# Weight chunks made straight from the raw weights, and one index search for both halves of a head

## The chip, the cores and the metric

The kernel runs on one core of a Trainium2 chip. The metric is device time in microseconds from one launch to its end. Five engines work side by side, each through its own list of instructions in a fixed order: TensorE (PE, whose weight loads are listed as PEld), VectorE (DVE), ScalarE (ACT), GpSimd (POOL) and SyncE (SP, which issues most DMAs).

## The reference

A layer sums an attention part and a part with 4096 small experts, over 2048 tokens of width 512.

```python
xn = _layernorm(x)
out = x + _A_ref(xn, wq, wk, wv, wo) + _B_ref(xn, w_q, k1, k2, u, v)

# A: 32 heads of 16 for the queries, one shared head for keys and values
scores = einsum("bhqd,bkd->bhqk", q, k) * Dh ** -0.5
o = einsum("bhqk,bkd->bhqd", softmax(scores), v)      # then @ wo

# B: for each token and each of 32 heads, with dk = 128 and E = 64
s1 = einsum("nhd,ed->nhe", q1, k1)                     # 64 scores, first half
s2 = einsum("nhd,ed->nhe", q2, k2)                     # 64 scores, second half
i1, i2 = the two best of each;  t1, t2 their scores
cand = t1 + t2 (four sums);  the best two of these name two experts i1 * 64 + i2
g = softmax(of the two sums)
act = gelu(xn . u[expert])
out += g * act * v[expert]
```

## The kernel before

**Two streams.** The attention is a loop of 256 steps, each with eight `sc` products (L450), four exponentials (L457) and the `pv` products (L467). Its units set the pace. A second stream, the score thread, is dealt in between the steps: a fixed amount of its estimated cost (`yield` values, in us) for each step, so that it ends with the attention. All lists of instructions are written out ahead by this program; nothing is reordered at run time.

**The score thread** works on items. An item is one tile of 128 tokens times one chunk of four expert heads: twelve `psc` products (L701) give 128 x 512 scores in PSUM, eight groups of 64 (four heads, two halves). VectorE finds the eight largest of each group (L714, MAX8) and their places (L716, which the chip runs as a load of the eight values and a find). Four items make a `batch`: VectorE adds up the pair sums, POOL turns the places (`fi`, L760) into expert numbers, ACT takes an exponential and VectorE forms the gates. There are 128 items and 32 batches.

**The weight chunks.** The scores need w_q and the keys multiplied together, 512 x 512 for each of eight chunks. `wp_make` (L630 to 670) does this: for each of four heads two products `pw` (L646) with the keys `kTs` as the stationary side, a copy to SBUF by ACT (`wt`, L647), then for each quarter of the depth four transposes `pwt` (L659), from which ACT (L661) and VectorE (L662) form a high and a low f16 half. Chunks 0 and 1 are made at the start, 2 to 7 among the items of the first token group. The raw weights come by `wp_load` (L607) into `wqt` tiles; `wp_square` (L617) and `wp_factors` (L624) give a scale for each chunk from their squares.

**Experts.** For half of the tokens (the first two groups) each chosen expert is one slot of 128 tokens: an indirect DMA on POOL gathers 128 rows of u and v (L1181), VectorE multiplies u with the tokens (a dot, L1193), four slots share a short chain (`gq`, `gy`, `ga`, L1202 to 1204, a tanh on ACT and `w`, L1216), and VectorE adds v times the weight to the sum (an add, L1228). There are 512 slots; line 1591 sets how many a step gets. For the other two groups all 4096 experts are computed: one-hot products first, then a dense stage of `pact` (L917) and `pout` (L1059) products with splits on ACT and VectorE.

So the run has a start, then making chunks beside items and slots (A), items and slots (B), the first one-hot part and dense stage, items and slots again (C1, C2), the second one-hot part and the last dense stage. The guard at L383 reads a flag on every engine and branches past a fallback.

Of the kernel before, what the change touches and what calls it, by code (L numbers as in the profile page):

```python
# [60 lines left out]
def tile_kernel(ctx, tc, x, wq, wkv, wo, wqT, kT, uv, ub, vb, out):  # L61
# [570 lines left out]
    def wp_make(c):  # L632

        wt = [big.tile([P, 2, 512], F32, name="wt", tag="da", bufs=2) for _ in range(2)]
        for h in range(4):
            for n in range(4 * c + h + 1, min(4 * c + h + 5, 4 * NC) if late[0] else 4):
                if ("raw", n // 4, n % 4) not in WC:
                    wp_load(n // 4, n % 4)
            if c == 2 and h > 1:
                wp_square()  # L640
            if c > 2 and h == 1:
                wp_factors()
            w = WC.pop(("raw", c, h))
            p = xtile("pw")
            for s in range(2):
                nc.tensor.matmul(p[s * E:(s + 1) * E, :], kTs[:, s, :], w[:, s, :], start=True, stop=True)  # L646
            nc.scalar.copy(wt[h // 2][:, h % 2, :], p)  # L647
            yield 0.9
        WC[c] = []
        if c == 2:  # L650
            yield 0.05
            wp_factors()
            yield 0.05
        for k in range(KC):
            for _ in range((0, 2, 1, 1)[k] if 1 < c < NC - 1 else 0):
                wp_square()
            p = xtile("pwt")
            for h in range(4):
                nc.tensor.transpose(p[:, h * P:(h + 1) * P], wt[h // 2][:, h % 2, k * P:(k + 1) * P], ident)  # L659
            wk = wk_tile()  # L660
            nc.scalar.activation(wk[:, 0, :], p, AF.Copy, scale=col(S_W + c))  # L661
            low = lambda p=p, wk=wk: nc.vector.scalar_tensor_tensor(wk[:, 1, :], p, col(S_W + c), wk[:, 0, :],  # L662
                                                                    op0=OP.mult, op1=OP.subtract)
            if c == 1 and late[0] is None:
                AFTER.append(low)
            else:
                low()
            WC[c].append(wk)
            (store if c > 1 else BULK.append)(lambda k=k, wk=wk: nc.sync.dma_start(d_w[c][:, k], raw(wk[:])))
            yield 0.45  # L670

# [9 lines left out]
    BT = 4  # L681

    def item(n_, ti, make=()):
# [5 lines left out]
        if jb == 0:  # L689
            m8 = small.tile([P, BT, 8, 8], F32, name="m8", bufs=1)  # L690
            i8 = small.tile([P, BT, 8, 8], U32, name="i8", bufs=1)
            M8[ph, c, b], I8[ph, c, b] = m8, i8
# [20 lines left out]
        for s in range(8):  # L713
            nc.vector.max(m8[:, jb, s, :], p[:, s * E:(s + 1) * E])  # L714
        for s in range(8):
            nc.vector.max_index(i8[:, jb, s, :], m8[:, jb, s, :], p[:, s * E:(s + 1) * E])  # L716
# [16 lines left out]
    def batch(ph, c, b):  # L733
# [3 lines left out]
        mv = m8.rearrange("p t (h s) k -> p t h s k", s=2)  # L737
        a1, a2, b1, b2 = mv[:, :, :, 0, 0], mv[:, :, :, 0, 1], mv[:, :, :, 1, 0], mv[:, :, :, 1, 1]
# [19 lines left out]
        fi = T("fi", F32, [P, BT, 8, 2])  # L758
        G_ = V if ph >= NSP and c == NC - 1 else nc.gpsimd
        G_.tensor_copy(fi, i8[:, :, :, 0:2])  # L760
        fv = fi.rearrange("p t (h s) k -> p t h s k", s=2)
# [4 lines left out]
        if ph < NSP:  # L766
# [12 lines left out]
            def gates():  # L779
                V.tensor_scalar(den, ex, 2.0 * XUP, 2.0 * XUP, op0=OP.mult, op1=OP.add)  # L780
# [29 lines left out]
        def gates():  # L810
            V.tensor_scalar(den, ex, 2.0, 2.0, op0=OP.mult, op1=OP.add)
# [764 lines left out]
    with tc.manual_schedule(engines=ENGINES):  # L1576
# [6 lines left out]
        for d in range(half + 24):  # L1583
# [71 lines left out]
            att_steps(d, mid, fill)  # L1655
        flush()
# [12 lines left out]
def build(nc, tc, args):  # L1669
    tile_kernel(tc, *args)  # L1670
# [33 lines left out]
```

## Time and profile before

| | |
|---|---|
| three timed runs | median 1787.16 us (1787.01 to 1787.59) |
| the profiled execution | 1783.53 us, span 1781.7 us |
| PE busy | 1690.9 us, 95% |
| VectorE busy | 1592.7 us, 89% |
| ScalarE busy | 1329.0 us, 75% |
| GpSimd busy | 680.8 us, 38% |
| mean granted TensorE clock | 0.994 |

Busy time on PE includes the tail of each product, so back-to-back products overlap in it: a `psc` product lasts 381 ns on the mean, while fifteen in a row take about 3.34 us. Read shares by stretch, not over the whole span. A row of instructions gives line, engine, operation, output and inputs with their shape, count, then busy time and mean ns, then idle time ahead of it and what ended it. A row of the time order gives start and length in us; where the start of the next row comes before the end of the last one, the two overlap in the pipeline.

### The profile page before, as it was taken

The numbers are of one execution on the slowest core, as the hardware profiler recorded it, in microseconds if no ns is written. First come the engines' busy times: TensorE is split into PE (matmuls) and PEld (weight loads), VectorE is DVE, ScalarE is ACT, GpSimd is POOL, SyncE is SP. The second block draws the span as 40 slices with busy tenths as digits, with TensorE's granted clock in tenths as the row PEclk, the third lists the DMA queues.
The fourth block names the chain that finished last, engine by engine and source line by source line (L and its number), as shares of the span: only waits on it lengthen the run. The fifth ranks groups of instructions, "written<-read, shape, count | busy, mean of one in ns | idle before, by whom it ended". The sixth has DMA issues, their size and how long they took to land.

```text
span 1781.7 us, 35035 instructions
## 1 busy us (share of the span) xinstructions
PE 1690.9 (95%) x11070; PEld 598.6 (34%) x11070; DVE 1592.7 (89%) x6367; ACT 1329.0 (75%) x1793; POOL 680.8 (38%) x893
## 2 busy tenths in 40 slices
PE   7989998999998889999999999999988899999998
PEld 3433333333333333333333333333333333333332
DVE  7748889999999977999998999999999779999995
ACT  6468787877776987888887666666669887777774
POOL 1024444445542002344343554545530124555450
PEclk9999999999999999999999999999999999999999
DMA  7378788999773469999999987767544679999993
GB/s 261 126 235 313 267 280 298 298 331 330 258 264 105 155 214 281 318 318 344 331 334 347 344 278 250 238 223 238 162 140 135 228 229 332 329 322 342 321 309 142
DMA packets 257272, 470.97 MB, mean 264 GB/s; under 512 B 107316, under 2 KB 118596, under 8 KB 257084
## 3 DMA queue, kind: packets, MB, share of 16 engines
q0 software_dynamic: 73728, 268.47, 43.7%
q1 hardware_dynamic: 182940, 199.59, 35.0%
q8 instruction: 87, 1.43, 0.3%
q14 instruction: 101, 0.83, 0.1%
q10 hardware_dynamic: 416, 0.66, 0.1%
HBM read 407.36 MB, written 56.39 MB: 260 GB/s over the span
## 4 chain that ended last, share of the span: by engine, by line
PE 47%; DVE 31%; ACT 8%; issue 4%; DMA 3%; SPq 1%; POOL 0%; ACTq 0%; DVEq 0%; POOLq 0%
PE pv L467 14%; PE sc L450 8%; PE pout L1059 8%; DVE i L716 7%; PE pact L917 7%; PE psc L701 5%; ACT pt L457 5%; DVE m L714 5%; DVE xa L1228 5%; DVE g L1193 4%; DVE oh L975 3%; PE pwo L567 2%; PE pw L646 1%; DVE obs L977 1%; DVE obs L978 1%
## 5 line engine op out<-in xcount | busy, mean ns | idle before, releaser
L457 ACT ACTIVATE pt<-sc 128x1024 f32<-128x1024 f32 x1024 | 990.2, 1026 | 327.6 <-PE sc L450 276.8
L1181 POOL DMA_INDIRECT g<-in_uv_dram,idx x512 | 550.3, 1075 | 867.2 <-DVE xa L1228 398.0
L467 PE MATMUL pv<-pt,vaug 128*32 128x512 f32 x4096 | 496.2, 602 | 0.0
L1228 DVE SCALAR_TENSOR_TENSOR xa<-g,w,xa 128x512 f32<-128x512 f32 x512 | 374.2, 747 | 0.1
L701 PE MATMUL psc<-wk,xt 128*128 128x512 f16 x1536 | 358.0, 381 | 7.8 <-DVE wk L662 4.7
L450 PE MATMUL sc<-qa,kaug 64*128 64x512 f16 x2048 | 323.1, 382 | 39.1 <-ACT pt L457 34.4
L1193 DVE CUSTOM_DVE_ANT_0 g<-g,xa 128x512 f32<-128x512 f32 x512 | 335.1, 684 | 12.6 <-DMA g<-in_uv_dram,idx 12.3
L701 PEld LDWEIGHTS <-xt 128*128 128x128 f16 x1536 | 141.2, 98 | 205.5 <-issue 57.2
L450 PEld LDWEIGHTS <-kaug 64*128 64x128 f16 x2048 | 82.9, 94 | 377.5 <-issue 373.5
L716 DVE FIND_INDEX8 i<-m,psc 128x8 uint32<-128x64 f32 x1024 | 206.9, 226 | 0.0
L467 PEld LDWEIGHTS pv<-pt,vaug 128*32 128x32 f32 x4096 | 107.3, 109 | 253.4 <-issue 253.4
L917 PE MATMUL pact<-xt,wk 128*128 128x512 f16 x768 | 181.9, 382 | 0.0
L1059 PE MATMUL pout<-wk,wd 128*128 128x512 f16 x768 | 175.8, 379 | 0.0
L714 DVE MAX8 m<-psc 128x8 f32<-128x64 f32 x1024 | 146.3, 217 | 6.5 <-PE psc L701 6.2
L1059 PEld LDWEIGHTS <-wd 128*128 128x128 f16 x768 | 73.1, 98 | 92.5 <-issue 8.1
L917 PEld LDWEIGHTS <-wk 128*128 128x128 f16 x768 | 69.1, 98 | 99.5 <-issue 27.1
L975 DVE TENSOR_TENSOR oh<-io,tr 128x2048 f16<-128x2048 f16 x64 | 78.0, 1218 | 4.9 <-PE pg L1013 4.8
L716 DVE MATCH_VALUE_LOAD i<-m,psc 128x8 f32 x1024 | 76.7, 75 | 0.0
L760 POOL CAST fi<-i 128x64 f32<-128x64 uint32 x30 | 8.2, 272 | 147.2 <-DVE i L716 143.7
L1062 DVE SCALAR_TENSOR_TENSOR da<-pout,cols,da 128x512 f32<-128x512 f32 x72 | 53.1, 745 | 6.3 <-PE pout L1059 4.9
L1132 DVE SCALAR_TENSOR_TENSOR gy<-gy,pact 128x512 f32<-128x512 f32 x60 | 40.9, 681 | 17.4 <-ACT gy L1131 17.4
L1131 ACT ACTIVATE gy<-pact,cols 128x512 f32<-128x512 f32 x60 | 41.7, 696 | 15.3 <-PE pact L917 14.4
(227 smaller groups left out, 1458.7 us busy)
## 6 DMA issues: line engine op xcount, KB each, us to landing
wk<-dw SPq DMA_DIRECT2D x96, 256.0 KB
wqt<-in_wqT_dram SPq DMA_DIRECT2D x32, 512.0 KB
un<-in_uv_dram SPq DMA_DIRECT2D x16, 1024.0 KB
ds<-wk SPq DMA_DIRECT2D x64, 256.0 KB
gates<-dg SPq DMA_DIRECT2D x64, 256.0 KB
wk<-ds SPq DMA_DIRECT2D x64, 256.0 KB
dg<-gst SPq DMA_DIRECT2D x14, 928.0 KB
dw<-wk SPq DMA_DIRECT2D x32, 256.0 KB
```

The source lines that it names most:

```text
L450: nc.tensor.matmul(p[:, b, :], kaug[o:o + 64, kc * P:(kc + 1) * P], QA[u][o:o + 64, i, :], start=True, stop=True)
L457: nc.scalar.activation(PT[u, kc, i], p, AF.Exp, scale=SCALE)
L467: nc.tensor.matmul(PV[u][32 * j:32 * j + 32, :], vaug[:, kc, :], pt[:, b, :], start=kc == 0, stop=kc == 15)
L701: nc.tensor.matmul(p, XT[kk][:, a, j * P:(j + 1) * P], WC[n_][kk][:, bb, :], start=n == 0, stop=n == 11)
L714: nc.vector.max(m8[:, jb, s, :], p[:, s * E:(s + 1) * E])
L716: nc.vector.max_index(i8[:, jb, s, :], m8[:, jb, s, :], p[:, s * E:(s + 1) * E])
L917: nc.tensor.matmul(p, us[:, a, k * P:(k + 1) * P], XT[k][:, c, :], start=n == 0, stop=n == 11)
L975: nc.vector.tensor_tensor(out=oa, in0=num(P), in1=bc(0, tb, P), op=OP.is_equal)
L1059: nc.tensor.matmul(p, wd[0][:, a, j * P:(j + 1) * P], vs[:, c, :], start=n == 0, stop=n == last)
L1181: nc.gpsimd.indirect_dma_start(out=gt, out_offset=None, in_=uv, in_offset=bass.IndirectOffsetOnAxis(ap=IDX[ph, c, ti][:, s:s + 1], axis=0))
L1193: nc.vector.tensor_tensor_reduce(u, u, XN[TPH * ph + ti], scale=1.0, scalar=0.0, op0=OP.mult, op1=OP.add, accum_out=a[:, i:i + 1])
L1228: nc.vector.scalar_tensor_tensor(acc, v, w[:, i:i + 1], acc, op0=OP.mult, op1=OP.add)
```

## The change

**Weights.** Chunks 2 to 7 are made by `wp_direct`. The raw weights are the stationary side and the keys the moving one, so that each of 32 products (four quarters of the depth, four heads, two halves) gives its 128 x 64 part of `pwt` in the place where it is wanted. The products `pw`, their copies and the transposes are gone for these chunks. A chunk's four raw tiles are kept until its last quarter; `wp_load` has eight buffers for them in place of five. The squares and loads are dealt out in other places.

**Search.** The eight values of a head's second half are written from slot 6 of sixteen, over the last two of the first half, and one `max_index` for the head looks for eight values (six and two) in 128 scores. Places of the second half then count from 64; `over` takes 64 off. Where a value of the second half is also in the first, the place comes out below 64: `most` keeps a mark of it, `met_flag` turns it into a flag, and at the end `build` reads the flag on every engine and, if it is set, runs the whole program again with the old search.

**Rates.** Line 1669 deals slots to steps at 2.7, 2.5 and 2.1 in place of 2.5, 2.3 and 1.75.

```diff
     def wp_load(c, h):
         n = 4 * c + h
-        if n < 2 or n > 7 and (n - 8) % 5 < 2:
+        if n < 2 or n > 7 and (n - 8) % 8 < 2:
             w = big.tile([P, 2, D], F32, name="wqt", tag="wqt", bufs=2)
...
+        elif (n - 8) % 8 < 5:
+            w = late[0].tile([P, 2, D], F32, name="wqt", tag="gy", bufs=3)
         else:
-            w = late[0].tile([P, 2, D], F32, name="wqt", tag="gy", bufs=3)
+            w = big.tile([P, 2, D], F32, name="wqt", tag="oh", bufs=3)
...
+    def wp_direct(c):
+        ahead = [(c + 1, h) for h in range(4)] if c < NC - 1 else []
+        WC[c] = []
+
+        def make(k):
+            p = xtile("pwt")
+            for h in range(4):
+                w = WC["raw", c, h]
+                for s in range(2):
+                    nc.tensor.matmul(p[:, h * P + s * E:h * P + (s + 1) * E], w[:, s, k * P:(k + 1) * P], kTs[:, s, :],
+                                     start=True, stop=True)
+            wp_halves(c, k, p)
...
+        make(0)
+        load(2)
+        yield 1.3
+        load(3)
...
+        make(1)
+        square()
+        yield 1.3
...
+    SECOND = 8 if exact else 6
+    most = const.tile([P, BT, 4, 2], F32, name="most")
...
         for s in range(8):
-            nc.vector.max(m8[:, jb, s, :], p[:, s * E:(s + 1) * E])
-        for s in range(8):
-            nc.vector.max_index(i8[:, jb, s, :], m8[:, jb, s, :], p[:, s * E:(s + 1) * E])
+            nc.vector.max(m8[:, jb, s // 2, SECOND * (s % 2):][:, :8], p[:, s * E:(s + 1) * E])
+        if exact:
...
+        else:
+            for h in range(4):
+                nc.vector.max_index(i8[:, jb, h, :8], m8[:, jb, h, :8], p[:, h * P:(h + 1) * P])
...
+        for s in range(2):
+            G_.tensor_copy(fv[:, :, :, s, :], i8[:, :, :, SECOND * s:SECOND * s + 2])
+        if not exact:
+            over = T("over", F32, [P, BT, 4, 2])
+            G_.tensor_scalar(over, fv[:, :, :, 1, :], float(E), -float(E), op0=OP.is_ge, op1=OP.mult)
+            G_.tensor_add(fv[:, :, :, 1, :], fv[:, :, :, 1, :], over)
+
+        def meet():
+            if not exact:
+                V.tensor_max(most, most, over)
...
-            make = wp_make(n + 1) if 0 < n < NC - 1 else iter(())
+            make = wp_direct(n + 1) if 0 < n < NC - 1 else iter(())
...
-                pos += (2.5 if len(IDX) < NC * TPH else 2.3 if 0 <= d - since < 20 else 1.75, 0, 0.25, 1.5, 0.5)[dense_on[0]]
+                pos += (2.7 if len(IDX) < NC * TPH else 2.5 if 0 <= d - since < 20 else 2.1, 0, 0.25, 1.5, 0.5)[dense_on[0]]
...
+            if d == half - 8 and not exact:
+                met_flag()
...
+    with tc.tile_pool(name="met", bufs=1) as met:
+        flag = met.tile([1, 1], I32, name="met")
+        tile_kernel(tc, False, flag, *args)
+        again = nc.values_load(flag[0:1, 0:1], min_val=0, max_val=1)
+        with tc.If(again != 0):
+            tile_kernel(tc, True, None, *args)
```

VectorE's list at an item of B before: eight MAX that wait only for PE, eight searches, then a dot (`ISA g,act`, with the read of its sum). In brackets stand the semaphores that an instruction waits for; DVE is the engine's own.

```order
L714 MAX m_5951<-psc 128x8 [waits PE_49]
L714 MAX m_5951<-psc 128x8 x7
L716 MAX_INDEX i_5952<-m_5951,psc 128x8 [waits DVE_49] x8
L1193 ISA g,act<-g,xa 128x512 [waits DMASW0_49]
L1193 ISA act 128x1
```

The end of the same item now:

```order
L777 MAX m_5879<-psc 128x8
L777 MAX m_5879<-psc 128x8 [waits DVE_49]
L777 MAX m_5879<-psc 128x8
L777 MAX m_5879<-psc 128x8 [waits DVE_49]
L784 MAX_INDEX i_5880<-m_5879,psc 128x8 x3
L784 MAX_INDEX i_5880<-m_5879,psc 128x8 [waits DVE_49]
L1271 ISA g,act<-g,xa 128x512 [waits DMASW3_49]
L1271 ISA act 128x1
```

Four searches are gone, and of each pair of MAX the second waits for the first; the value waited for is the one that the MAX just ahead sets. Before, the value that a search waited for was set by the MAX eight places ahead.

VectorE's list between two items of B before (`gq`, `gy` and `ga` are the chain of four slots):

```order
L1193 ISA g,act<-g,xa 128x512 [waits DMASW2_49]
L1193 ISA act 128x1
L1193 ISA g,act<-g,xa 128x512 [waits DMASW3_49]
L1193 ISA act 128x1
L1228 SCALAR_TENSOR_TENSOR xa<-g,w,xa 128x512
L1202 SCALAR_TENSOR_TENSOR gq<-act 128x4 [waits DVE_49]
L1203 SCALAR_TENSOR_TENSOR gy<-gq,act 128x4 [waits DVE_49]
L1204 TENSOR_TENSOR ga<-act,gg 128x4
```

And after, at the same place:

```order
L1271 ISA g,act<-g,xa 128x512 [waits DMASW5_49]
L1271 ISA act 128x1
L1271 ISA g,act<-g,xa 128x512 [waits DMASW6_49]
L1271 ISA act 128x1
L1294 SCALAR_TENSOR_TENSOR w<-gth,ga 128x4 [waits Activation_49]
L1271 ISA g,act<-g,xa 128x512 [waits DMASW7_49]
L1271 ISA act 128x1
L1306 SCALAR_TENSOR_TENSOR xa<-g,w,xa 128x512 [waits DVE_49]
L1280 SCALAR_TENSOR_TENSOR gq<-act 128x4 [waits DVE_49]
L1306 SCALAR_TENSOR_TENSOR xa<-g,w,xa 128x512
L1281 SCALAR_TENSOR_TENSOR gy<-gq,act 128x4 [waits DVE_49]
L1306 SCALAR_TENSOR_TENSOR xa<-g,w,xa 128x512
```

Three dots and three adds stand where two dots and one add stood.

PE's list in A before, one quarter's transposes among the `psc` products:

```order
L701 MATMUL psc<-wk,xt 128x512
L701 LDWEIGHTS xt
L701 MATMUL psc<-wk,xt 128x512
L659 MATMUL pwt<-ident,wt 128x128 [waits DVE_49]
L659 MATMUL pwt<-ident,wt 128x128 x3
L701 LDWEIGHTS xt
```

And after, a quarter's eight products, ahead of the attention's next `sc`:

```order
L764 LDWEIGHTS xt
L764 MATMUL psc<-wk,xt 128x512
L674 MATMUL pwt<-kTs,wqt 128x64 [waits DVE_49]
L674 MATMUL pwt<-kTs,wqt 128x64 x7
L451 LDWEIGHTS kaug [waits DMAHW6_49,DMAHW5_49,DMAHW4_49]
L451 MATMUL sc<-qa_203,kaug 128x512 [waits Activation_49]
```

The weight load of an f32 product is not a row of its own in the list.

More of the change, by code (lines that the diff above doesn't have):

```diff
@@ L60, in tile_kernel @@
 @with_exitstack
-def tile_kernel(ctx, tc, x, wq, wkv, wo, wqT, kT, uv, ub, vb, out):
+def tile_kernel(ctx, tc, exact, flag, x, wq, wkv, wo, wqT, kT, uv, ub, vb, out):
     nc = tc.nc
@@ new lines, in wp_direct, with load @@
+    def wp_direct(c):
[8 more added lines that the diff above has]
+                                     start=True, stop=True)
+            wp_halves(c, k, p)
+            if k == KC - 1:
+                for h in range(4):
+                    WC.pop(("raw", c, h))
+        def load(h, c=c):
+            if c + 1 < NC and ("raw", c + 1, h) not in WC:
+                wp_load(c + 1, h)
+        square = wp_square if ahead else lambda: None
+        if c == 2:
+            load(1)
+            wp_square()
+            yield 0.05
+            load(2)
+            wp_square()
+            yield 0.05
+            load(3)
+            wp_factors()
+            yield 0.05
+            yield 0.05
+        make(0)
+        load(2)
+        yield 1.3
+        load(3)
+        if c == 2:
+            square()
+        yield 0.05
+        make(1)
+        square()
+        yield 1.3
+        square()
+        yield 0.05
+        make(2)
+        square()
+        yield 1.3
+        if c > 2:
+            square()
+        yield 0.05
+        if ahead:
+            wp_factors()
+        make(3)
+        yield 1.3
+        load(0, c + 1)
+        load(1, c + 1)
+        yield 0.05
@@ L681, in tile_kernel, with met_flag @@
     BT = 4
+    SECOND = 8 if exact else 6
+    most = const.tile([P, BT, 4, 2], F32, name="most")
+    nc.vector.memset(most, -float(E))
+    def met_flag():
+        m = small.tile([P, 1], F32, name="mm", bufs=1)
+        nc.vector.reduce_max(m, most.rearrange("p t h k -> p (t h k)"), axis=AX.X)
+        p = xtile("pm")
+        nc.tensor.transpose(p[:1, :P], m, ident)
+        r = small.tile([1, 1], F32, name="prd", bufs=1)
+        nc.vector.reduce_max(r, p[:1, :P], axis=AX.X)
+        nc.vector.tensor_scalar(flag, r, 0.0, None, op0=OP.is_ge)
     def item(n_, ti, make=()):
@@ L779, in gates @@
             def gates():
+                meet()
                 V.tensor_scalar(den, ex, 2.0 * XUP, 2.0 * XUP, op0=OP.mult, op1=OP.add)
@@ L810, in gates @@
         def gates():
+            meet()
             V.tensor_scalar(den, ex, 2.0, 2.0, op0=OP.mult, op1=OP.add)
```

52 lines of the change are left out of this document (20 added, 32 removed).

## The prediction

> **What bounds the kernel now.** I read the engine totals first, then the span in seven stretches cut where the work changes, then single instructions in order of time, and the waits last.
>
> ```profile
> span 1781.7 us, 35035 instructions
> PE 1690.9 (95%) x11070; PEld 598.6 (34%) x11070; DVE 1592.7 (89%) x6367; ACT 1329.0 (75%) x1793; POOL 680.8 (38%) x893
> ```
>
> PE looks like the bound, but VectorE is close behind, and a mean over the span hides who waits where. The stretches say more (columns: window, its length, then busy time of PE, PEld, DVE, ACT and POOL):
>
> ```profile
> 123.00:350.00 227.00, 213.64 (x1324) 75.02 (x1324) 201.56 (x1032) 181.61 (x264) 103.37 (x133) 0.98 0.85 288
> 350.00:558.00 208.00, 204.46 (x1264) 69.33 (x1263) 204.99 (x1336) 155.38 (x210) 102.58 (x190) 1.00 0.83 281
> 558.00:1018.00 460.00, 429.50 (x3057) 150.65 (x3056) 412.58 (x948) 382.52 (x511) 146.74 (x134) 0.99 0.86 286
> 1018.00:1174.00 156.00, 156.00 (x931) 52.71 (x929) 151.29 (x893) 97.17 (x119) 78.51 (x108) 1.00 0.77 264
> 1174.00:1326.00 152.00, 150.98 (x941) 51.02 (x937) 149.17 (x985) 97.83 (x119) 75.11 (x144) 1.00 0.58 188
> 1326.00:1420.00 94.00, 78.95 (x975) 33.42 (x979) 85.13 (x154) 82.84 (x101) 11.65 (x8) 1.00 0.51 166
> 1420.00:1750.00 330.00, 328.27 (x1993) 110.65 (x1989) 298.52 (x743) 254.00 (x340) 148.48 (x136) 1.00 0.95 310
> ```
>
> The rows are, in order: A, where the weight chunks are still made (attention steps 1 to 32); B, items and expert slots without making (33 to 64); the first dense stage; C1 and C2, items and slots again (137 to 160, 161 to 184); the second one-hot part; the last dense stage. In A every engine has room. In B and C2 PE and DVE are both full: DVE idles 208.00 - 204.99 = 3.0 us in B and 2.8 us in C2, so work added to DVE there lengthens the stretch almost in full, and work taken from it alone gains nothing, since PE has only 3.5 and 1.0 us of room. In the last dense stage PE is full and DVE has 31 us to spare.
>
> PE hardly waits for DVE so far; this is the row that will grow if DVE becomes the longer engine (waits of PE in 350 to 558):
>
> ```profile
> PE psc L701 <- DVE i L716: 2.2, 2, 1.1
> ```
>
> **The change, the search.** One item searches eight groups of 64. Before, its eight MAX8 follow each other freely and its eight load-and-find pairs too:
>
> ```profile
> 380.78 1.15 DVE L714 MAX8 m<-psc 128x8 f32<-128x64 f32 x8
> 381.83 0.08 DVE L716 MATCH_VALUE_LOAD i<-m,psc 128x8 f32 x1
> 382.03 0.08 DVE L716 MATCH_VALUE_LOAD i<-m,psc 128x8 f32 x1
> ...
> 383.43 0.34 DVE L505 RECIPROCAL rc<-rc 128x32 f32<-128x32 f32 x1
> ...
> L714 DVE MAX8 m<-psc 128x8 f32<-128x64 f32 x1024 | 146.3, 217 | 6.5 <-PE psc L701 6.2 <-issue 0.2
> L716 DVE FIND_INDEX8 i<-m,psc 128x8 uint32<-128x64 f32 x1024 | 206.9, 226 | 0.0
> ```
>
> From 380.78 to 383.43 is 2.65 us: eight MAX8 in 1.05 (0.131 apart, though one lasts 0.217) and eight pairs in 1.60 (0.200 apart). After, four pairs go. No row shows a find over 128 elements. It can't be under 0.200 a pair, nor over 0.400. I take 0.267: 64 more elements at the slope between a 16-element and a 512-element operation, (0.69 - 0.17) / 496 = 1.05 ns each (0.17 is L747 and 0.69 is L1193, both below). Four pairs: 1.07, a gain of 0.53.
>
> But in the new order every second MAX8 waits for the one in front of it, because it overwrites two of its slots. What a DVE instruction costs that waits for its predecessor:
>
> ```profile
> 380.39 0.17 DVE L744 TENSOR_TENSOR cond<-c,c 128x16 f32<-128x16 f32 x1
> 380.48 0.17 DVE L746 TENSOR_TENSOR mx<-c,c 128x16 f32<-128x16 f32 x1
> 380.69 0.17 DVE L747 TENSOR_TENSOR mx<-mx,s 128x16 f32<-128x16 f32 x1
> 384.89 0.17 DVE L1202 SCALAR_TENSOR_TENSOR gq<-act 128x4 f32<-128x4 f32 x1
> 385.09 0.16 DVE L1203 SCALAR_TENSOR_TENSOR gy<-gq,act 128x4 f32<-128x4 f32 x1
> 385.17 0.16 DVE L1204 TENSOR_TENSOR ga<-act,gg 128x4 f32<-128x4 f32 x1
> ```
>
> L746 needs nothing of L744 and starts 0.09 behind it; L747 needs L746 and starts 0.21 behind it, 0.04 after its end. L1203 and L1204 show the same. So a waiting MAX8 starts 0.217 + 0.04 = 0.257 behind its predecessor in place of 0.131: 0.126 more, four times an item, 0.50. The new item is 4 x (0.257 + 0.131) + 1.07 = 2.62 us: 0.03 less than 2.65. The search gains next to nothing. With a find pair at its ends the item is 2.35 to 3.15.
>
> The Trainium skill says otherwise ("VectorE: DVE Perf Modes", section "The DRAIN you can't avoid"): the flush between two operations comes anyway, and "the semaphore costs nothing extra here". By it the item would be 2.12. The rows above, 0.21 against 0.09, disagree for these short operations, and I go by the rows.
>
> The small additions: `meet` is one more DVE operation for each of 32 batches, about 0.1 each between neighbours; the extra conversions lie on POOL, which is 38% busy.
>
> **The change, the rates.** Slots are dealt to steps faster until the last dense stage. In the two programs' order steps 33 to 64 hold 58 dots and 58 adds before, 68 and 69 after; steps 161 to 184 hold 40 and 41 before, 48 and 50 after; 137 to 160, 51 and 54 against 56 and 56; 1 to 32, 75 and 70 against 81 and 75. The first dense stage keeps its number, and the last one loses about 30 of each. What one costs:
>
> ```profile
> 474.10 0.69 DVE L1193 CUSTOM_DVE_ANT_0 g<-g,xa 128x512 f32<-128x512 f32 x1
> 474.71 0.16 DVE L1202 SCALAR_TENSOR_TENSOR gq<-act 128x4 f32<-128x4 f32 x1
> 475.06 0.23 DVE L714 MAX8 m<-psc 128x8 f32<-128x64 f32 x1
> 390.43 1.41 DVE L1228 SCALAR_TENSOR_TENSOR xa<-g,w,xa 128x512 f32<-128x512 f32 x2
> 391.75 0.23 DVE L714 MAX8 m<-psc 128x8 f32<-128x64 f32 x1
> ```
>
> A dot takes 0.61, an add (391.75 - 390.43) / 2 = 0.66, and four slots share a chain of 0.35 and a weighing of 0.10. B gets 10 x 0.61 + 11 x 0.66 + 2.6 x 0.45 = 14.6 us more, less 0.03 for each of its items, plus 1.0 for ten `meet`: items by stretch are these MAX8 counts over eight,
>
> ```profile
> 123.00:350.00 227.00, 29.75 (x208) 0.98 0.85 288
> 350.00:558.00 208.00, 47.44 (x333) 1.00 0.83 281
> 1018.00:1174.00 156.00, 29.49 (x208) 1.00 0.77 264
> 1174.00:1326.00 152.00, 34.22 (x240) 1.00 0.58 188
> ```
>
> so 14.6 - 1.2 + 1.0 = 14.4 against 3.0 of room: **B +11.4**. C2: 8 x 0.61 + 9 x 0.66 + 0.9 = 11.8, - 0.9 + 0.8 = 11.7 against 2.8: **C2 +8.9**. C1: 4.8 - 0.8 + 0.6 = 4.6 against 4.7: **0**. The last dense stage sheds some 40 us of DVE that nobody waits for; PE has 1.7 us of room there: **-1**.
>
> **The change, the weights.** Six chunks are made the new way.
>
> ```profile
> 306.94 0.95 PE L624 MATMUL pn<-squares,ones_f 128*128 128x1 f32 x8
> 307.81 1.08 PE L646 MATMUL pw<-wqt,kTs 128*64 128x512 f32 x4
> 308.82 0.39 PE L701 MATMUL psc<-wk,xt 128*128 128x512 f16 x1
> 320.92 0.60 PE L659 MATMUL pwt<-ident,wt 128*128 128x128 f32 x4
> 321.35 0.38 PE L701 MATMUL psc<-wk,xt 128*128 128x512 f16 x1
> ...
> L659 PEld LDWEIGHTS pwt<-ident,wt 128*128 128x128 f32 x128 | 15.2, 143 | 12.3 <-issue 3.8 <-DVE flag L378 1.6 <-DVE i L716 1.3
> ...
> L647 ACT COPY wt<-pw 128x512 f32<-128x512 f32 x32 | 18.6, 589 | 14.4 <-PE pw L646 10.8 <-issue 3.5
> ```
>
> Old, a chunk: four pairs of products at 1.01 (308.82 - 307.81, four passes) and four sets of transposes at 0.43: 5.8 us of PE. New: 32 products in two passes each (as the trace shows for `pw` and `pn`), each pass with its own 128x128 f32 weights and only 64 columns. The nearest row is `pn`, the same weights with one column: eight in 0.87, 0.109 a pass. 64 passes are 7.0 us, 1.2 more. The ends: if only columns counted, 1.01 / 4 x 64 / 512 = 0.03 a pass, 2.0 a chunk; and if a load's time stood alone it could reach the 0.143 that a transpose's load lasts, 9.2 a chunk. Over six chunks: +7, between -23 and +20. The Trainium skill ("TensorE: Matmul & The Clock Gate", section "Back-to-back issue gap") has about 81 ns for a load-and-product pair of 128 columns. By it the term would be -4.
>
> Against that ACT loses 24 copies x 0.589 = 14 us in A, and PE and ACT one exchange a head. A has 13.4 us of PE idle time, and part of it is such exchanges, so I take **A +4**, between -18 (then DVE's 201.56 and the 7.6 of A's own extra slots, 6 x 0.61 + 5 x 0.66 + 0.6, bind) and +20. The weight loads from HBM keep their number and size; now eight buffers hold two whole chunks, and a chunk's next loads wait for its last product, with some 30 us until they are used, against transfers of 512 KB each. Nothing there should bind; were that cover gone, SP's later loads would queue behind.
>
> **The end.** All engines read a flag and branch past a second copy of the program. The guard that is there already shows the price:
>
> ```profile
> 120.36 0.20 DVE L378 TENSOR_SCALAR flag<-prd,cols 1x1 int32<-1x1 f32 x1
> 121.59 0.30 PE L659 MATMUL pwt<-ident,wt 128*128 128x128 f32 x1 [1.42 <-PEq L383]
> ```
>
> 1.0 us from flag to next work. At the end it can run beside the last stores; with the flag's own transpose on PE I take **+1**, from 0 to 4.
>
> Sum: 11.4 + 8.9 + 0 - 1 + 4 + 1 = +24.3. The profiled execution took 1783.53 us, of which the span is 1781.7; the three timed runs have a median of 1787.16, and the difference is laid on that: **1811 us**.
>
> **Rivals.** *The waits cost nothing* (the skill's rule above): an item of 2.12 frees 22 us in B and 16 in C2, the new slots fill 15.6 and 12.6 of it, and PE binds as before. What is left is A and the end: 1787 + 4 + 1 - 2 = **1790**. For it: the dealt slots would just fit. Against it: L747 and L1203.
>
> *VectorE is really relieved* (the other side): if a find pair over 128 costs no more than over 64 and the waits vanish in the pipeline, the item is 1.05 + 0.80 = 1.85. The place is A: DVE there falls by 26 x 0.80 = 21 and rises by 7.6, so PE stops waiting, and its idle 13.4 us shrink to B's share, 4; B and C2 give their 3.5 and 1.0. With the weights at +7: 1787 - 9 - 4.5 + 7 + 1 = **1781**, and less with cheaper weight passes, down to some 1765. It decides as soon as the item is under about 2.1.
>
> *The flag is set*: two searched values of a head are equal to the last bit and the whole program runs again, about **3570**.
>
> **Chances.** Forecast 0.62, free waits 0.20, relief 0.16, second run 0.02. Range: the forecast's own unknowns give 1797 to 1832 (A and the find pair above all); to hold 8 in 10 it goes from 1774, into the relief case, to 1830. About 0.2%, 3.6 us, is what can be told from no change. Faster: 0.15 of relief and 0.03 of free waits, 0.18; within: 0.10 of free waits and 0.01, 0.11; slower: 0.71.
>
> **What would show it.** MAX8 of an item spread to about 1.55 us, in steps of 0.13 and 0.26; find pairs 0.267 apart; waits of PE's `psc` for DVE up from 2.2 us in B to some 10; B near 219 us and C2 near 161; eight new weight products in about 1.75 us; DVE under 80% in the last dense stage, with PE as full as before. I am wrong if MAX8 stays 0.13 apart throughout, or if A shrinks by more than 10 us.

## The result, and the profile after

The changed kernel took 1842.7 us (median of four runs, 1841.0 to 1849.8), the kernel before 1787.4 beside it: a ratio of 1.033, 95% interval 1.031 to 1.035. The forecast was 1811, at most 1830. The sign was right; +24 was forecast and +55 came. The first profile of the changed kernel is of its longest execution (1849.8, span 1848.0). A second one (the run e10 below) has a span of 1842.3; the stretches are taken from that one, single instructions from the first.

The engines' totals, and the chain that ended last, of the first profile:

```profile
span 1848.0 us, 34486 instructions
PE 1714.4 (93%) x11263; PEld 631.4 (34%) x11263; DVE 1585.9 (86%) x5385; ACT 1317.4 (71%) x1769; POOL 703.0 (38%) x983
...
PE 45%; DVE 34%; ACT 8%; issue 5%; DMA 1%; SPq 0%; another core or an unknown queue 0%; ACTq 0%; DVEq 0%
```

VectorE has a thousand instructions fewer and is 6.8 us less busy, in a span 66 us longer. One item, as VectorE runs it:

```profile
384.82 1.69 DVE L777 MAX8 m<-psc 128x8 f32<-128x64 f32 x8
386.42 0.07 DVE L784 MATCH_VALUE_LOAD i<-m,psc 128x8 f32 x1
386.48 0.29 DVE L784 FIND_INDEX8 i<-m,psc 128x8 uint32<-128x128 f32 x1
386.69 0.07 DVE L784 MATCH_VALUE_LOAD i<-m,psc 128x8 f32 x1
...
387.48 0.68 DVE L1271 CUSTOM_DVE_ANT_0 g<-g,xa 128x512 f32<-128x512 f32 x1
```

MAX8 take 386.42 - 384.82 = 1.60 us (1.05 before), the four finds 387.48 - 386.42 = 1.06 (1.60 before): 2.66 in all. The item costs VectorE what it cost before.

Stretches of the second profile, in the columns of the first table: steps 1 to 32 (A), 33 to 64 (B), 137 to 160 (C1) and 161 to 184 (C2):

```profile
112.00:360.00 248.00, 230.60 (x1551) 108.53 (x1548) 211.77 (x865) 174.75 (x252) 117.06 (x158) 0.97 0.83 285
360.00:582.00 222.00, 207.93 (x1258) 69.34 (x1257) 213.28 (x1051) 155.35 (x213) 121.60 (x230) 0.98 0.83 284
1052.00:1212.00 160.00, 154.58 (x919) 51.84 (x918) 151.91 (x694) 96.52 (x120) 86.23 (x130) 1.00 0.77 257
1212.00:1380.00 168.00, 157.27 (x948) 51.69 (x946) 161.12 (x804) 99.53 (x123) 93.26 (x176) 0.98 0.61 201
```

VectorE still sets the pace in B and C2. Its idle time there, 222.00 - 213.28 = 8.7 us and 168.00 - 161.12 = 6.9 us, is nearly all made of gaps of 0.03 to 0.11 us ahead of instructions that depend on a neighbour. Of the idle times over 0.15 us, which a list of waits shows, B has one of 0.2 us and C2 none. VectorE's MAX8 in B (busy time, mean, then idle time ahead of them), its one listed wait in B, and its longest listed wait in C1:

```profile
L777 DVE MAX8 m<-psc 128x8 f32<-128x64 f32 x328 | 63.5, 225 | 5.8 <-issue 0.2
```

```profile
DVE m L777 <- issue: 0.2, 1, 0.2
```

```profile
DVE w L1294 <- ACT gth L1287: 3.2, 2, 2.2
```

So the waits inside the items (5.8 us in B) count as idle time, and VectorE's lower busy time does not mean that it had room. In C1, 3.2 of its 8.1 us are two waits for the tanh. It is PE, nearly full before, that now waits. Of the whole second profile, what PE waited for most:

```profile
PE sc L451 <- ACT pt L458: 60.6, 88, 8.0
PE psc L764 <- DVE i L784: 15.3, 11, 3.3
```

Length of each stretch by the exponentials that end it (four to a step, read to 2 us), in us; chips are named by letters in the runs' order:

| kernel | chip | A | B | -80 | -120 | -136 | C1 | C2 | -208 | -256 |
|---|---|---|---|---|---|---|---|---|---|---|
| before | | 236 | 208 | 86 | 266 | 108 | 154 | 154 | 130 | 308 |
| changed (e10) | S | 248 | 222 | 88 | 264 | 118 | 160 | 168 | 134 | 308 |
| e1 old rates | Q | 232 | 210 | 86 | 266 | 106 | 156 | 156 | 132 | 312 |
| e2 rates alone | Q | 236 | 226 | 86 | 268 | 114 | 156 | 168 | 130 | 308 |
| e3 weights alone | Q | 234 | 206 | 88 | 264 | 108 | 154 | 156 | 132 | 308 |
| e4 firsts first | Q | 238 | 206 | 84 | 268 | 118 | 154 | 152 | 130 | 308 |
| e5 same, old rates | R | 234 | 204 | 82 | 264 | 108 | 154 | 152 | 130 | 312 |
| e6 e4, dense rate | R | 238 | 208 | 84 | 268 | 106 | 154 | 152 | 128 | 310 |
| e7 e4, other queue | R | 236 | 206 | 82 | 264 | 114 | 154 | 152 | 128 | 308 |
| e8 changed, old weights | R | 234 | 226 | 86 | 268 | 116 | 158 | 166 | 134 | 308 |
| e13 changed, dense rate | T | 244 | 222 | 88 | 270 | 106 | 174 | 168 | 132 | 310 |
| e14 = e5 | T | 244 | 208 | 82 | 264 | 106 | 154 | 154 | 128 | 312 |

### The profile page after: what moved, and what is told of

Same layout as the page of the kernel before. It is cut to its first block, busy times and chain, and to the rows that moved or that the text cites. A ratio compares the mean times of both kernels' runs of the same rounds, so it can differ in the third digit from the quotient of the medians.

```text
span 1848.0 us, 34486 instructions
## 1 busy us (share of the span) xinstructions
PE 1714.4 (93%) x11263; PEld 631.4 (34%) x11263; DVE 1585.9 (86%) x5385; ACT 1317.4 (71%) x1769; POOL 703.0 (38%) x983
## 4 chain that ended last, share of the span: by engine, by line
PE 45%; DVE 34%; ACT 8%; issue 5%; DMA 1%; SPq 0%; another core or an unknown queue 0%; ACTq 0%; DVEq 0%
PE pv L468 13%; PE sc L451 8%; DVE m L777 8%; PE pout L1137 7%; PE pact L995 7%; DVE xa L1306 7%; DVE i L784 6%; DVE g L1271 6%; ACT pt L458 5%; PE psc L764 3%; PE pwo L568 2%; PE pwt L674 2%; DVE oh L1053 2%; DMA rw<-in_vb_dram 1%; ACT wk L954 1%
## 5 line engine op out<-in xcount | busy, mean ns | idle before, releaser
L1259 POOL DMA_INDIRECT g<-in_uv_dram,idx x512 | 540.6, 1056 | 926.1 <-DVE xa L1306 397.6
L468 PE MATMUL pv<-pt,vaug 128*32 128x512 f32 x4096 | 502.6, 609 | 0.0
L451 PE MATMUL sc<-qa,kaug 64*128 64x512 f16 x2048 | 329.0, 384 | 71.2 <-ACT pt L458 63.6
L777 DVE MAX8 m<-psc 128x8 f32<-128x64 f32 x1024 | 197.7, 224 | 23.5 <-PE psc L764 5.2
L784 DVE FIND_INDEX8 i<-m,psc 128x8 uint32<-128x128 f32 x512 | 139.1, 290 | 0.0
L1294 DVE SCALAR_TENSOR_TENSOR w<-gth,ga 128x4 f32<-128x4 f32 x128 | 20.7, 161 | 46.2 <-ACT gth L1287 46.0
L828 POOL CAST fi<-i 128x32 f32<-128x32 uint32 x60 | 12.2, 231 | 120.9 <-DVE i L784 119.9
L1189 DVE SCALAR_TENSOR_TENSOR gy<-gy,gates 128x512 f32<-128x512 f32 x60 | 41.3, 688 | 16.0 <-ACT gy L1211 15.2
```

The source lines that it names most:

```text
L451: nc.tensor.matmul(p[:, b, :], kaug[o:o + 64, kc * P:(kc + 1) * P], QA[u][o:o + 64, i, :], start=True, stop=True)
L468: nc.tensor.matmul(PV[u][32 * j:32 * j + 32, :], vaug[:, kc, :], pt[:, b, :], start=kc == 0, stop=kc == 15)
L777: nc.vector.max(m8[:, jb, s // 2, SECOND * (s % 2):][:, :8], p[:, s * E:(s + 1) * E])
L784: nc.vector.max_index(i8[:, jb, h, :8], m8[:, jb, h, :8], p[:, h * P:(h + 1) * P])
L1259: nc.gpsimd.indirect_dma_start(out=gt, out_offset=None, in_=uv, in_offset=bass.IndirectOffsetOnAxis(ap=IDX[ph, c, ti][:, s:s + 1], axis=0))
```

## The experiments

**Which part costs.** Theory R: the new rates put more slots beside a search that got no shorter. Rivals: the weights, or the search itself.

e1 is the changed kernel with the old rates:

```diff
-                pos += (2.7 if len(IDX) < NC * TPH else 2.5 if 0 <= d - since < 20 else 2.1, 0, 0.25, 1.5, 0.5)[dense_on[0]]
+                pos += (2.5 if len(IDX) < NC * TPH else 2.3 if 0 <= d - since < 20 else 1.75, 0, 0.25, 1.5, 0.5)[dense_on[0]]
```

> Both edits kept, the slots dealt at the old rates 2.5, 2.3, 1.75. Theory R (the rates overfill VectorE, since the search frees nothing): B and C2 come back to about 208 and 152 us, C1 to 156, the stall of the first dense stage is gone, and only A stays about 12 us longer: 1798 to 1804 us. Rival W (the new search and the flag are themselves dear, whatever the rates): still above 1825.

Measured: 1792.3, ratio 1.0045 (1.0025 to 1.0065), 6 us below theory R's range: B, C1, C2 and the dense stage came back as it said, but A took 232 and not 12 us more. e2 is the reverse, the kernel before with the new rates and nothing else:

> The kernel before with the new rates and nothing else. Theory R: an item costs VectorE 2.65 us in both searches, so B, C1 and C2 lengthen as in the changed kernel (about 12 + 8 + 10 us) and the first dense stage may stall as there (10 us): 1815 to 1830 us, with A as before. Rival W: the rates alone do little, 1787 to 1795.

Measured: 1827.0, ratio 1.0243 (1.0225 to 1.0260). Theory R holds: one line of numbers, alone, costs some 44 us. Its B, C1 and C2:

```profile
350.00:576.00 226.00, 210.50 (x1260) 69.33 (x1258) 219.02 (x1371) 155.41 (x213) 114.47 (x200) 0.97 0.85 284
1044.00:1200.00 156.00, 154.03 (x919) 51.72 (x918) 153.57 (x885) 96.39 (x120) 82.53 (x111) 1.00 0.80 265
1200.00:1368.00 168.00, 155.94 (x949) 51.90 (x947) 165.15 (x1047) 99.29 (x123) 87.40 (x155) 0.99 0.62 202
```

In B VectorE got 219.02 - 204.99 = 14.0 us of work, as the forecast had worked out for the slots (14.6), but the stretch grew by 18: VectorE's idle time rose from 3.0 to 7.0 where it was to go to nothing. The 3.0 before were 67 gaps of 0.03 to 0.11 us between instructions, with no listed wait among them, and added work can't fill these. They are 2.9 us here too, and the other 4.1 are waits:

```profile
DVE on L516 <- DMA rsb<-dinv: 2.0, 1, 2.0
DVE m L714 <- PE psc L701: 1.7, 2, 1.0
DVE cond L744 <- POOL fi L760: 0.5, 1, 0.5
```

In C2, where no wait is listed, the idle time simply stayed: 2.8 before, 168.00 - 165.15 = 2.85 here.

e3 is the changed kernel with the search as before, the old rates (as in e1) and no second copy, so that only the weights are new:

```diff
-        tile_kernel(tc, False, flag, *args)
-        again = nc.values_load(flag[0:1, 0:1], min_val=0, max_val=1)
-        with tc.If(again != 0):
-            tile_kernel(tc, True, None, *args)
+        tile_kernel(tc, True, None, *args)
```

> Chunks 2 to 7 straight from the raw weights, with the old search, the old rates and no second copy. Theory R: A about 12 us longer (46 us of short products for 35 of the old ones), the rest as before: 1797 to 1802 us. Rival S (the longer A comes from the search and its slots): 1787 within 3 us.

Measured: 1785.9, ratio 1.0015 (0.9998 to 1.0031). Rival S holds, and theory R's price for the weights was too high: here they cost next to nothing. A quarter's sixteen passes take what was forecast (first profile of the changed kernel):

```profile
135.27 1.89 PE L674 MATMUL pwt<-kTs,wqt 128*128 128x64 f32 x16
137.10 0.60 PE L451 MATMUL sc<-qa,kaug 64*128 64x512 f16 x4
```

137.10 - 135.27 is 1.83 us, 0.114 a pass; 22 of the 24 quarters take 1.73 to 1.84, and all of them 43.4 us, where the old way took 6 x 5.8 = 35. Against that stands what ACT gives: in the 236 us of A before it is busy 188.24, in e3's 234 us 175.02.

**The waiting MAX8.** e4 is the changed kernel, its new rates too, with one line in another order. Each second-half MAX8 still overwrites the slots of its first half, but four instructions back, not one:

```diff
-        for s in range(8):
+        for s in (0, 2, 4, 6, 1, 3, 5, 7):
             nc.vector.max(m8[:, jb, s // 2, SECOND * (s % 2):][:, :8], p[:, s * E:(s + 1) * E])
```

> The changed kernel with the eight MAX8 of an item in another order, the four first halves and then the four second ones, so that the one a MAX8 waits for stands four places ahead. Theory R: the wait is over before it is reached, an item is 1.05 + 1.07 = 2.1 us, VectorE gets 0.53 us an item back (22 us in B, 16 in C2), B and C2 return to 208 and 152 us or a little under; A's 12 us and the dense stall stay: 1800 to 1812 us. Rival W (the wait costs nothing, the find or the flag does): 1835 to 1843.

Measured: 1790.5, ratio 1.0035 (1.0016 to 1.0054), 52 us less than the changed kernel and below what either theory expected. Some 10 of the 52 lie in A (238 against 248), which the new order does not explain: see steps 1 to 32 below. About 40 are the order's. The same item in e4:

```profile
384.02 1.14 DVE L777 MAX8 m<-psc 128x8 f32<-128x64 f32 x8
385.08 0.07 DVE L784 MATCH_VALUE_LOAD i<-m,psc 128x8 f32 x1
...
386.14 0.67 DVE L1271 CUSTOM_DVE_ANT_0 g<-g,xa 128x512 f32<-128x512 f32 x1
```

Its B, in the columns of the stretches, and the shares of its chain:

```profile
350.00:556.00 206.00, 203.93 (x1257) 68.69 (x1257) 199.10 (x1065) 154.76 (x213) 126.85 (x230) 0.99 0.90 310
```

```profile
PE 69%; DVE 9%; ACT 8%; DMA 4%; issue 2%; SPq 0%; ACTq 0%; DVEq 0%; POOLq 0%
```

Eight MAX8 take 1.06 us in place of 1.60: (1.60 - 1.06) / 4 = 0.135 for each wait on the instruction just ahead. The item is 2.12, B falls from 222 to 206 with the same slots in it, PE's waits of `psc` for VectorE are gone, and VectorE's share of the chain is 9% in place of 34%. This is the whole loss of B and C2, shown by order alone.

e5 is e4 with the old rates:

> The changed kernel with two edits: an item's MAX8 in the order (0, 2, 4, 6, 1, 3, 5, 7), so that none overwrites what the instruction just ahead of it wrote, and the search's old rates (2.5/2.3/1.75 slots a step). Theory D (the new rates move the switch to the second token group into the dense stage; that and the end are all that is left once the MAX8 do not wait): the dense stage (steps 121-136) at 106-108 us as with the old rates, B and C2 206 and 152, total 1781-1787, below the 1792.3 of the old rates with the waiting order. Rival N (the order only pays where DVE is full, so at the old rates nothing is left to gain): 1790-1794, B 210 and C2 156 as with the waiting order.

Measured: 1776.2, ratio 0.9960 (0.9946 to 0.9973). The stages are those of theory D, the total is 5 us below its range. The rates that cost 44 us with the old item cost some 13 without the wait (1.0035 against 0.9960, on two chips), 10 of them in the dense stage. (e14 below qualifies the gain of e5.)

**The first dense stage (steps 121 to 136).** It takes 118 us in the changed kernel and in e4, 108 before. In the changed kernel's chain of waits stands, where the second token group begins:

```profile
948.39 6.30 DMA out_dram<-xa
...
955.08 0.43 SPq L1366
...
955.62 0.45 SPq L912
956.07 0.04 issue
956.12 10.22 DMA rw<-in_vb_dram
...
966.99 1.93 ACT pt L458 x2
```

SP's list holds the reload of `xa` (L1365, L1366), which must wait until the output has left that tile, and behind it the stage's raw loads `rw` (L912, L913). At the old rates the group changes after the last of the raw loads: before, the last `rw` is issued at 948.7 us and the first of the output stores at 953.0, while in the second profile of the changed kernel the stores begin at 933.9 and four of the five pairs of raw loads come from 951.3 on. Two edits of e4 move one of them. e6 deals the first half of the stage fewer slots, so that all raw loads come first; e7 issues the reload from POOL:

```diff
# e6
-                pos += 2.6 if d < half * 3 // 4 else max(0.0, NSL - pos) / max(half - 3 - d, 1)
+                pos += 2.2 if d < half * 3 // 4 else max(0.0, NSL - pos) / max(half - 3 - d, 1)
# e7
-        nc.sync.dma_start(xa[:, 1, :], d_xn[t - TPH])
-        nc.sync.dma_start(xa[:, 0, :], x[t * P:(t + 1) * P, :])
+        nc.gpsimd.dma_start(xa[:, 1, :], d_xn[t - TPH])
+        nc.gpsimd.dma_start(xa[:, 0, :], x[t * P:(t + 1) * P, :])
```

> The changed kernel with the MAX8 of a row's first halves first (it measured 1790.5) and the search's rate in the first half of the dense stage 2.2 slots a step in place of 2.6, so that all raw loads of the dense stage stand ahead of the reload of xa on SP's queue, as before the change. Theory D (the +10 us of steps 121-136 are raw loads queued behind a reload that waits for an output store): steps 121-136 at 107-110 us in place of 118, total 1779-1783. Rival P (the stage is longer because more search work lies in it, whatever the queue): steps 121-136 at 114 or more, total 1787-1793.

> The changed kernel with the MAX8 of a row's first halves first (1790.5), all rates as changed, and only the reload of xa for the second token group issued from GpSimd in place of SP, so that no raw load stands behind it. Theory D: steps 121-136 at 107-111 us in place of 118, total 1779-1784; the wait of wk for a raw load (6.9 us) is gone. Rival P: steps 121-136 stay at 116-120, total 1788-1793.

Measured: e6 1783.9, ratio 1.0000 (0.9988 to 1.0011), the stage 106; e7 1779.9, ratio 0.9991 (0.9969 to 1.0014), the stage 114, between its two theories. Waits of ACT in the stage, first e4, then e7:

```profile
ACT wk L954 <- DMA rw<-in_ub_dram: 6.9, 1, 6.9
```

```profile
ACT wk L954 <- DMA rw<-in_ub_dram: 2.7, 2, 2.6
```

So the queue is part of it: with the reload on POOL the longest wait for a raw load goes from 6.9 us to 2.6, and the stage loses 4. The stage in the kernel before, in e7 and in e6 (the last two columns are the DMA engines' share and GB/s):

```profile
910.00:1018.00 108.00, 104.45 (x633) 34.84 (x632) 98.33 (x237) 84.20 (x114) 45.88 (x42) 0.98 0.98 334
```

```profile
902.00:1016.00 114.00, 106.91 (x639) 35.55 (x638) 99.73 (x242) 84.99 (x114) 51.62 (x51) 0.97 0.97 334
```

```profile
910.00:1016.00 106.00, 102.25 (x630) 34.43 (x628) 89.88 (x214) 83.87 (x111) 38.98 (x37) 1.00 0.94 313
```

Rival P's added work isn't in the stage: VectorE is busy for 98.33 us before and 99.73 in e7, and the kernel before, e5 and e4 all deal it 41 dots, and take 108, 108 and 118. What the 6 us are that e7 does not get back isn't shown. Before and in e7 the DMA engines are full, at the same 334 GB/s; bytes are rate by time, 36.1 MB before and 38.1 in e7, and 2.0 MB / 334 GB/s = 6.0 us would fit. But in e7 the output stores still stand on SP ahead of four pairs of raw loads, and that isn't told apart. e6 gets all of it back, with all raw loads ahead of the reload, but it also takes work out of the stage: 37 gathers in place of 42, 89.88 us of VectorE and 33.2 MB.

e13 makes e6's edit in the changed kernel, with its waiting MAX8:

> The changed kernel (1842.7; MAX8 waiting, new rates) with one edit: 2.2 slots a step in place of 2.6 in the first half of the dense stage, so that its raw loads stand ahead of the reload of xa on SP's queue. Theory D: steps 121-136 at 106-110 us in place of 118, total 1831-1837. Rival P (DVE is the bound around it, so the time comes back in the steps behind): 1839-1845.

Measured: 1846.7, ratio 1.0342 (1.0319 to 1.0366). The stage is 106 as theory D said, and nothing is won: C1 grew to 174, and the total is above even the rival's range. Steps 121 to 184 take 118 + 160 + 168 = 446 us in the changed kernel and 448 here. The rival's reason isn't borne out: C1 holds 57 dots here and 56 in the changed kernel, and what grew are VectorE's waits there, of which the changed kernel had only the 3.2 us shown above:

```profile
DVE w L1294 <- ACT gth L1287: 9.4, 4, 2.9
DVE m L777 <- PE psc L764: 5.0, 4, 1.6
```

Why these waits come isn't shown.

**Steps 1 to 32.** They take 12 us more in the changed kernel. Neither the rates alone (e2, 236) nor the weights alone (e3, 234) nor weights and waiting search together (e1, 232) show it. e8 is the changed kernel with the old `wp_make`:

> The changed kernel (waiting MAX8, new rates, 1842.7) with the weights made the old way (copies and transposes). Theory K (the +12 us of steps 1-32 need the new weights: 16 products in one go ahead of the exponentials behind them on PE, and the wk halves ahead of them on ACT): steps 1-32 at 236-240 us, total 1829-1836. Rival L (they come from the waiting search at the higher rate alone): steps 1-32 at 245-250, total 1840-1846.

Measured: 1831.5, ratio 1.0278 (1.0250 to 1.0306), A 234: theory K, so it seemed, the weights in company. e10 ran the changed kernel again:

> The changed kernel once more, for a second profile: the first was of an execution of 1849.8 us, 7-8 us above its three others. Theory A (steps 1-32 take 12 us more in every execution): steps 1-32 at 245-249 us in an execution of 1840-1844. Rival O (the 7-8 us of that execution lay in steps 1-32): steps 1-32 at 238-242, the other stages as in the first profile.

Measured: 1845.9, ratio 1.0337 (1.0291 to 1.0383), A 248: it was no single execution. But e14, the program of e5 once more on chip T, took 244 in A where e5 took 234 on chip R:

> The fastest so far (new weights, search of a row's 128 scores with the MAX8 of the first halves first, old rates; 0.996 of before) beside two variants of it on one chip: 0.995-0.998 of before.

Measured: 1794.0, ratio 1.0048 (1.0027 to 1.0069): the same program, and outside the interval of e5. Rows of A and of its waits, first e5, then e14:

```profile
114.00:348.00 234.00, 224.14 (x1543) 106.96 (x1542) 195.52 (x846) 174.05 (x250) 110.92 (x152) 0.99 0.84 289
```

```profile
PE sc L451 <- ACT pt L458: 6.4, 16, 0.5
```

```profile
114.00:358.00 244.00, 226.18 (x1537) 107.32 (x1536) 194.66 (x843) 173.66 (x251) 107.63 (x152) 0.98 0.82 279
```

```profile
PE sc L451 <- ACT pt L458: 13.5, 21, 2.0
...
ACT wk L655 <- PE sc L451: 12.0, 4, 3.3
```

The work is the same. In the slower one ACT's `wk` four times waits up to 3.3 us for PE, and exponentials stand behind it in ACT's list. All twelve profiles of kernels with the new weights are of one kind or the other: 232 to 238 on chips Q and R (e1, e3 to e7), 244 to 248 on S and T and in the first pair (whose chip isn't known). The six kernels with the old weights, on every chip, take 234 to 238. So the new weights leave A open to a pattern that lasts some 10 us longer, and which one comes goes by the chip in these runs. Each chip held one batch of runs, so chip and time can't be told apart. Why isn't shown; e8's A of 234 on chip R therefore doesn't tell that search and weights cost together, as theory K had it.

**The end, and what is left.** e9 changes the search alone (old weights and rates); e11 is e5 with the old weights, and e16 the same program on chip T; e12 is e5 without the flag and the second copy, and e15 the same on chip T:

```diff
# e12, e15
-            if d == half - 8 and not exact:
-                met_flag()
...
-        again = nc.values_load(flag[0:1, 0:1], min_val=0, max_val=1)
-        with tc.If(again != 0):
-            tile_kernel(tc, True, None, *args)
```

> The kernel before with only the search changed (MAX8 in the waiting order, search of a row's 128 scores at once, flag and second copy of the program), old weights and old rates. Theory E (an item costs DVE as much as before, and the new weights are worth 0 to +3 us at the old rates, so what is left of the 1792.3 with both is the end): 1787-1791, every stage within 3 us of before, the time from the last exponential to the end 3-4 us longer. Rival X (weights and waiting search only cost together, as they did at the new rates, 1842.7 against 1831.5): 1780-1784.

> As the kernel with the MAX8 of a row's first halves first and the old rates (1776.2), with the weights made the old way (copies and transposes). Theory N (the 11 us that TensorE gets with the new weights lie beside ACT's relief in steps 1-32, and cost nothing): 1773-1779, steps 1-32 at 233-237. Rival B (with VectorE relieved, TensorE is the bound, and the old weights' 11 us less of it show): 1764-1771, steps 1-32 at 223-228.

> As the kernel with the MAX8 of a row's first halves first and the old rates (1776.2), without the flag's reduction, the read of the flag at the end and the second copy of the program (left out: the run again where a value is met twice). Theory F (the second copy costs what the time from the last exponential to the end shows, 20.6 us against 17.7, and the flag's reduction a wait of 2 us on TensorE): 1771-1774. Rival Z (it costs nothing): 1775-1778.

> The fastest so far without the flag's reduction, the read of the flag and the second copy (left out: the run again where a value is met twice). Theory F (they cost 3-5 us): 3-5 us below the kernel with them on the same chip. Rival Z: within 2 us of it.

> The fastest so far with the weights made the old way. Theory G (the new weights pay where nothing waits for VectorE: ACT's relief of 13 us in steps 1-32 against TensorE's 11 us more): 5-12 us above the fastest on the same chip. Rival N (they are worth nothing either way, and the difference so far was the chips'): within 3 us of it.

| | chip R | chip S | chip T |
|---|---|---|---|
| e5, e14 | 0.9960 (0.9946-0.9973) | | 1.0048 (1.0027-1.0069) |
| without the second run: e12, e15 | | 0.9992 (0.9972-1.0011) | 0.9990 (0.9975-1.0005) |
| with old weights: e11, e16 | | 1.0022 (1.0005-1.0040) | 0.9996 (0.9978-1.0014) |

On chip T e15 is 10.6 us below e14 by the medians, but their profiled executions differ by 3.7 (spans 1782.5 and 1786.2), theory F's size: 4 in the last 48 steps (308 against 312), 3 behind them, less what other stages give back. The rest of the 10.6 isn't placed. The second copy itself shows in every profile: from the end of the last exponential to the end it is 20.6 to 21.4 us in the 13 with it and 18.2 to 18.3 in the five without. e11 and e12 (1789.7 and 1784.5) lie above the ranges of both their theories, which were set from 1776.2 on chip R; on chip S they had no partner. e16 is 10.7 below e14, with A at 238 against 244: theory G fails, and so does its rival's "within 3 us". e9 gave 1800.9, ratio 1.0073 (1.0043 to 1.0103), more than both its theories expected; its profile, of its longest execution, is longer in B by 2, C1 by 4, C2 by 2 and the last 48 steps by 6. Differences of some 0.5% between these kernels can't be told from the chips. Whether any version beats the kernel before stays open: e5 did on one chip, and didn't on another. That the changed kernel and e2 are slower by 2 to 3%, and that e4's order takes nearly all of it back, is far outside that.

## Why the prediction was wrong in size

Its steps against the second profile, in us of span:

| term | forecast | measured |
|---|---|---|
| item on VectorE | 2.62 | 2.66 |
| A, weights and 6 slots | +4 | +12 (-4 to +2 in e1 and e3 to e7) |
| B | +11.4 | +14 |
| first dense stage | 0 | +10 |
| C1 | 0 | +6 |
| C2 | +8.9 | +14 |
| second one-hot part | 0 | +4 |
| last dense stage | -1 | 0 |
| end | +1 | +2.6 (time behind the last exponential, 18.3 to 20.9) |

**The item was right,** by the right steps: MAX8 1.60 (forecast 1.55), finds 0.265 apart (0.267). The rows L746 and L747 on a dependent DVE instruction carried it: 0.126 forecast for a wait on the neighbour, 0.135 measured. The rule of the Trainium skill ("VectorE: DVE Perf Modes", section "The DRAIN you can't avoid"), by which the semaphore costs nothing extra, does not hold for this kernel's MAX8. Its item of 2.12 is what e4 measured, with the dependence four instructions back. The first rival, 1790, had the right price for its condition: e4 made it true and took 1790.5. That the totals agree so closely is partly luck: 10 us of e4 are the dense stage, which the rival did not have, and the kernel before took 1783.2 on e4's chip, not 1787.

**The work of the rates was right, the room was not.** This is the step that failed in B, C1 and C2. The forecast set VectorE's added work against its idle time (3.0 us in B, 2.8 in C2, 4.7 in C1) and took the rest as the loss. Most of that idle time could not be filled. In B and C2 it was gaps of 0.03 to 0.11 us between dependent instructions, which stay whatever is added; in C1, 3.2 of the 4.7 were two waits of `w` for the tanh,

```profile
DVE w L1216 <- ACT gth L1209: 3.2, 2, 2.4
```

and they are 3.2 us in the changed kernel as well. So the stretches grew by about the whole work: B by 14 where 14.4 was worked out, C2 by 14 (12.3 between the ends of the exponentials, read exactly) where it was 11.7, C1 by 6 where it was 4.6. The C1 term of 0 is this error at its plainest, though with the old item (e2) C1 did fill part of its room and grew by 2. The room taken off was 3.0 + 2.8 + 4.6 = 10.4 us. PE, which idles 14.1 us in B (3.5 before), only follows VectorE; its waits of `psc` for VectorE there are 5.1 us, where some 10 were forecast.

**The dense stage had no term.** This is the other step that failed, and worth 10 us, the largest term put at 0. The stage "keeps its number" of slots, and VectorE's work in it stays. But the rates move the change of token group, with its output stores and reloads, from behind the stage's raw loads to in front of four of their five pairs on SP's queue. The prediction had asked of each queue what is behind the weight loads, not what the reload of `xa` would stand in front of. e7 shows 4 of the 10 us to be the reload's place on SP's queue; e5, with the loads in the old order and the same 41 dots, has all 10 back, and e6 too, which also takes work out; what the other 6 of e7 are stays open. e13 shows that with the waiting MAX8 mending the stage alone brings nothing.

**The weights' term** had the right price: 0.109 a pass forecast, 0.108 to 0.115 measured, and about 8 us of PE where 7 were forecast, with no effect on e3's time. "TensorE: Matmul & The Clock Gate" (the Trainium skill, section "Back-to-back issue gap") would have had 81 ns; the pass here is a third longer or more. The +12 of A, 8 us above the forecast, is inside the bounds given for it, by a cause not foreseen and not cleared up. The +4 of the second one-hot part isn't explained either.

Room, dense stage and A make up 28 of the 36 us by which the span grew more than forecast (1842.3 - 1781.7 = 60.6 against 24.3). The range ended at 1830 because it summed the unknowns of single terms (A, the find) and took the room, C1 and the dense stage as sure.

## What to carry to other kernels

An instruction that overwrites what its neighbour has just written can pay for the wait (each such MAX8 0.135 us here); before a search, a merge or a copy is made shorter, look at the order in the row, and put such pairs some places apart (here one line, about 40 us). Before an engine's idle time is spent in a sum, list what it is made of: here it was gaps between dependent instructions and waits for another engine, which added work filled little of. When a schedule's rate is changed, list what else is tied to its counters, such as the change of a buffer, and look at which queue it now stands in, and in front of what.

## What the runs showed of the hardware that was not expected

- MAX8 over 64 elements are 0.13 us apart when free, and 0.135 longer when they depend on the neighbour; four instructions' distance hides it (eight in 1.06 us, 1.05 before). Such gaps are listed as idle time of an engine that has no room. A find with its load over 128 elements takes 0.265, over 64 0.200.
- A float32 product with 128x128 weights and 64 columns takes 0.108 to 0.115 us for each of its two passes in 22 of 24 quarters, against 0.109 with one column: up to 64, the columns hardly count. (A `pw` pass, with 512 columns, took 1.01 / 4 = 0.25.)
- The same program came out at 0.996 of the kernel before on one chip and at 1.005 on another, with intervals that don't touch, and 10 of the 12 us between the two profiles lay in A (234 against 244). An interval from runs on one chip did not hold on the next.
